# V's first weight slices over both DMA queues, with tile 1's steps one place earlier, in a fused attention and MLP block

## The chip, the cores and the metric

The kernel runs on one core of one Trainium2 chip. The metric is the device time of one execution in microseconds (us). The time before is the median of three runs.

## The reference

The input `x` has 2048 rows of 1024 values in bf16. The kernel computes a layer normalization, a sliding-window attention with 32 heads of 32, and a dense layer pair with silu, both with a residual.

```python
def _A_ref(x, wqkv, wo):
    qkv = (x @ wqkv)...          # q, k, v: 32 heads of 32
    scores = q k^T * 32 ** -0.5  # kept where 0 <= i - j < 256
    o = softmax(scores) @ v
    return o @ wo
def _B_ref(x, w1, w2):           # 1024 -> 3584 -> 1024
    return silu(x @ w1) @ w2

h = x + _A_ref(_layernorm(x), wqkv, wo)
h2 = h + _B_ref(_layernorm(h), w1, w2)
```

## The kernel before

The rows are worked on in four blocks of 512, each of four tiles of 128 rows. The order of the instructions of each engine is written out by hand. For every block the q, k and v groups are matmuls of 128x128 weights against 512 columns, eight per group, into one accumulator bank. The attention of a block is woven between the groups of the next one. Then come the output projection (`wo_group`, L268), the first dense layer (`h1_group`, L695) and the second (L732).

The change touches the beginning. SyncE's queue loads tile 0 of `x` (x0), then the eight slices of V's weights (wv0 to wv7: 128 rows of `wqkv`, all 1024 columns of V, 256 KB each), with tiles 2 and 3 (x2, x3) behind slices 3 and 4, and then 1 MB of the weights of q. ScalarE's queue loads tile 1 (x1) alone. Every one of these tiles and slices is 256 KB. ScalarE's instructions, its transfers among them, are issued in the order in which the program gives them; the same holds for SyncE.

The first two tiles are not normalized before the matmuls of V. TensorE transposes the raw tile (`turn`, L471), and the mean is taken off in the copies out of PSUM. The mean of tile 0 comes in two halves, one from ScalarE (`neg_mean`, L458) and one from VectorE (L502). The first two column blocks of a tile are centred by VectorE before they are transposed (`center_first`, L475; `turn_mid`, L479) and copied out (`copy_mid`, L482: VectorE for tile 0, ScalarE for tile 1). For the other six, the mean is spread over a row by two matmuls (`spread_mean`, L467), copied to SBUF (L513 for tile 0, L531 for tile 1), and added in `center` (L486). The variances are taken by ScalarE beside it (`var_first`, L491), and the root is multiplied in when V is copied out (L558).

The matmuls of V for tiles 0 and 1 (`slices`, L522) follow the list `FIRST`. An entry `(j, k)` is tile `j` against slice `k`: two matmuls of 512 columns. The entry `(1,)` is `turn_mid`, `copy_mid` and `spread_mean` of tile 1 with the work of ScalarE and VectorE behind them. An entry of four values transposes half of tile 2. After the list come V of tiles 2 and 3 (L237), and then the q and k groups of the first block (L247).

The banks of the accumulators are drawn by a counter:

```python
def next_acc():
    acc_n[0] += 1
    return acc_banks[acc_n[0] % len(acc_banks)]
```

`acc_banks` holds four banks during the first stage, two afterwards (`del acc_banks[2:]`, L569), and six from the first dense layer on: the four new ones (`hacc`) lie where the attention's scores lay, which ScalarE reads with the exponentials of L312 and L313.

Of the kernel before, what the change touches and what calls it, by code (L numbers as in the profile page):

```python
# [39 lines left out]
]  # L40
SPLIT = [(0, 8), (8, 16), (16, 21), (21, 27), (27, 32)]
FIRST = [
    (0, 0), (0, 1), (0, 2), (1,), (0, 3), (1, 0), (1, 1), (1, 2), (1, 3),
    (0, 4), (1, 4), (0, 5), (1, 5), (0, 6), (1, 6), (2, 0, 4, "turn"), (0, 7), (2, 4, 8, "turn"), (1, 7),
]

# [2 lines left out]
def kernel(  # L49
# [10 lines left out]
    nc = tc.nc  # L60
# [3 lines left out]
    S, D = x2d.shape  # L64
# [4 lines left out]
    KT = D // P  # L69
# [29 lines left out]
    def view(region, off, *dims):  # L99
        n = 1  # L100
        for d in dims:
            n *= d
        ap = region[:, off:off + n]
        if len(dims) == 2:
            return ap.rearrange("p (a b) -> p a b", b=dims[1])
        if len(dims) == 3:
            return ap.rearrange("p (a b c) -> p a b c", b=dims[1], c=dims[2])
        return ap

    wqk = view(r_w, 0, KT, 2 * D)  # L110
    wv = view(r_w, 16384, KT, D)
# [20 lines left out]
    wqkv_v = A_wqkv.rearrange("(kt p) n -> p kt n", p=P)  # L132
# [5 lines left out]
    def load_x(b, j, queue=nc.sync):  # L138
        queue.dma_start(out=x_ring[(b % 2) * 4 + j], in_=x2d[(b * 4 + j) * P:(b * 4 + j + 1) * P, :])

    def load_wqkv(c0, parts=1, queues=(nc.sync,)):
        dst = wqk[:, :, c0:c0 + 512] if c0 < 2 * D else wv[:, :, c0 - 2 * D:c0 - 2 * D + 512]
        n = KT // parts
        for k in range(0, KT, n):
            queues[k // n % len(queues)].dma_start(out=dst[:, k:k + n, :], in_=wqkv_v[:, k:k + n, c0:c0 + 512])
# [8 lines left out]

    load_x(0, 0)
    load_x(0, 1, nc.scalar)
    for k in range(KT):
        nc.sync.dma_start(out=wv[:, k, :], in_=wqkv_v[:, k, 2 * D:3 * D])
        if k in (3, 4):
            load_x(0, k - 1)  # L160
    load_wqkv(0)

    ident = const.tile([P, P], BF16, name="ident")
# [60 lines left out]
    acc_n = [0]  # L224
# [6 lines left out]
    def v_group(b, j, c, copy, between=None, acc=None):  # L231
        if acc is None:
            acc = next_acc()
        for kt in range(KT):
            if between:
                between(kt)
            nc.tensor.matmul(acc, lhsT=lnT_b[b % 2][:, kt, j * P:(j + 1) * P], rhs=wv[:, kt, c * 512:(c + 1) * 512],  # L237
                             start=(kt == 0), stop=(kt == KT - 1))
        copy(out=v[:, b * 4 + j, c * 16:(c + 1) * 16, 0:DH], in_=acc.rearrange("p (h d) -> p h d", d=DH))
# [327 lines left out]
    v_group(0, 3, 0, act)  # L567
    v_group(0, 3, 1, act)
    del acc_banks[2:]  # L569

    ps_tp.__exit__(None, None, None)
    ps_sc = tc.tile_pool(name="ps_sc", bufs=1, space=bass.MemoryType.PSUM, reuse_waits="tile")
# [212 lines left out]
```

## Time and profile before

| | |
|---|---|
| median of 3 runs | 691.5 us (691.18 to 691.62) |
| the profiled execution's own time | 691.33 us |
| its span | 689.6 us |
| granted TensorE clock | 1.000 |
| TensorE busy | 685.2 us (99%) |
| DMA moved | 61.48 MB, mean 89 GB/s |

The span goes from the first to the last instruction; the time is a little longer than the span. A row of the timeline gives the start, the time taken, the engine, the line, the operation, what is written and read, how many instructions are merged in it, and in brackets the idle time ahead of it and what ended that. `SPq` and `ACTq` are the issues of transfers on the queues of SyncE and ScalarE, `PE` is TensorE, `PEld` its weight loads, `DVE` VectorE, `ACT` ScalarE. A row of the waits gives the engine, what it writes, the line, whom it waited for, and then the total, the number of times and the longest.

### The profile page before, as it was taken

What the parts mean: (1) busy time and instruction counts of PE and PEld (TensorE: products, weight loads), DVE (VectorE), ACT (ScalarE), POOL (GpSimd) and SP (SyncE); (2) the same over time, 40 slices, a digit from 0 to 9 for tenths busy, and PEclk for the clock granted to TensorE, in tenths of its full rate; (3) what the DMA queues carried; (4) which work ended last, traced back from release to release, by engine and by line L of the source; (5) the groups of instructions that cost most, each with busy time, mean ns of one, the idle gap of its engine ahead of it and who ended that gap; (6) DMA issues with size and microseconds to landing.
All of it is one profiled execution on the core that took longest, in us unless ns stands there. A gap on an engine that the chain in (4) does not pass through costs nothing.

```text
span 689.6 us, 14236 instructions
## 1 busy us (share of the span) xinstructions
PE 685.2 (99%) x6008; PEld 343.0 (50%) x6008; DVE 291.3 (42%) x612; ACT 244.7 (35%) x462; POOL 160.6 (23%) x295
## 2 busy tenths in 40 slices
PE   9999999999999999999999999999999999999998
PEld 4445555555555555544444444444444444444445
DVE  5267647744444459444316133343133251333111
ACT  7326666667666766421310033300133100233000
POOL 1016665576666656400000000000000000000000
DMA  8842241136241888881023310032300124100110
GB/s 274 260 64 69 43 93 47 30 58 185 73 129 36 249 229 245 181 301 63 26 88 111 85 39 0 1 91 70 84 0 1 26 91 91 38 1 1 30 39 24
DMA packets 77648, 61.48 MB, mean 89 GB/s; under 512 B 52496, under 2 KB 60688, under 8 KB 77584
## 3 DMA queue, kind: packets, MB, share of 16 engines
q1 hardware_dynamic: 77440, 60.31, 31.9%
q8 instruction: 47, 0.77, 0.5%
q10 hardware_dynamic: 144, 0.26, 0.1%
q14 instruction: 17, 0.14, 0.1%
HBM read 39.85 MB, written 8.39 MB: 70 GB/s over the span
## 4 chain that ended last, share of the span: by engine, by line
PE 97%; DMA 1%; DVE 0%; ACT 0%; SPq 0%; issue 0%
PE hacc L695 19%; PE hacc L732 18%; PE acc L247 17%; PE acc L732 10%; PE acc L695 9%; PE acc L237 7%; PE acc L268 6%; PE o_ps L380 5%; PE sc L300 3%; PE hacc L268 1%; PE sc L352 1%; DMA r_w<-in_A_wqkv_dram 1%; PE sc L326 1%; PE tp L237 1%; PE acc L522 0%; PE o_ps L522 0%
## 5 line engine op out<-in xcount | busy, mean ns | idle before, releaser
L370 POOL TENSOR_SCALAR_AFFINE_SELECT r_e<-r_e 128x512 bf16<-128x512 bf16 (+1 forms) x288 | 157.6, 562 | 124.2 <-ACT r_e L360 60.4
L732 PEld LDWEIGHTS <-r_a 128*128 128x128 bf16 x952 | 90.9, 98 | 103.0
L695 PEld LDWEIGHTS <-r_w 128*128 128x128 bf16 x896 | 87.4, 98 | 105.2 <-issue 0.5
L732 PE MATMUL hacc<-r_a 128*128 128x512 bf16 (+1 forms) x588 | 124.1, 371 | 0.0
L695 PE MATMUL hacc<-r_e,r_w 128*128 128x512 bf16 x456 | 100.9, 379 | 0.0
L312 ACT ACTIVATE r_e<-sc 128x768 bf16<-128x768 f32 x96 | 78.2, 814 | 47.9 <-PE sc L300 46.9
L247 PEld LDWEIGHTS <-r_w 128*128 128x128 bf16 x512 | 47.1, 98 | 55.0 <-issue 1.0
L732 PE MATMUL acc<-r_a 128*128 128x512 bf16 (+2 forms) x364 | 72.6, 358 | 0.0
L704 ACT ACTIVATE r_n<-acc 128x512 f32<-128x512 f32 x15 | 9.0, 597 | 162.0 <-PE acc L695 162.0
L249 DVE CAST r_a<-acc 128x512 bf16<-128x512 f32 x56 | 38.7, 692 | 56.8 <-PE acc L247 56.5
L247 PE MATMUL acc<-r_t,r_w 128*128 128x512 bf16 x256 | 59.6, 380 | 0.0
L247 PE MATMUL acc<-r_w 128*128 128x512 bf16 x256 | 57.8, 380 | 0.0
L380 PEld LDWEIGHTS <-r_e 128*128 128x128 bf16 x1440 | 47.4, 96 | 17.9
L747 DVE SCALAR_TENSOR_TENSOR r_t<-hacc,r_t 128x512 bf16<-128x512 f32 (+1 forms) x21 | 14.1, 672 | 90.5 <-PE hacc L732 90.5
L268 PE MATMUL acc<-r_o,r_a 128*128 128x512 bf16 x216 | 50.9, 380 | 0.2
L695 PE MATMUL acc<-r_e,r_w 128*128 128x512 bf16 x216 | 49.1, 379 | 0.0
L380 PE MATMUL o_ps<-r_a,r_e 128*128 128x33 bf16 x1440 | 48.1, 178 | 0.0
L313 ACT ACTIVATE r_e<-sc 128x256 bf16<-128x256 f32 x96 | 37.6, 392 | 0.0
L268 PEld LDWEIGHTS <-r_a 128*128 128x128 bf16 x256 | 23.4, 98 | 27.4 <-issue 0.7
L695 PE MATMUL hacc<-r_a,r_w 128*128 128x512 bf16 x152 | 34.6, 379 | 0.2 <-ACT r_e L313 0.2
L705 DVE SCALAR_TENSOR_TENSOR r_a<-r_a,hacc 128x512 bf16<-128x512 f32 x30 | 20.6, 687 | 31.2 <-ACT r_a L704 31.2
L705 DVE SCALAR_TENSOR_TENSOR r_a<-r_n,hacc 128x512 bf16<-128x512 f32 x27 | 18.6, 687 | 28.1 <-ACT r_n L704 28.1
(106 smaller groups left out, 536.9 us busy)
## 6 DMA issues: line engine op xcount, KB each, us to landing
r_w<-in_B_w_dram SPq DMA_DIRECT2D x8, 896.0 KB, 6.2
r_a<-in_B_w_dram SPq DMA_DIRECT2D x7, 1024.0 KB, 8.0
r_w<-in_A_wqkv_dram SPq DMA_DIRECT2D x4, 1024.0 KB, 8.4
h_dram<-r_t SPq DMA_DIRECT2D x16, 256.0 KB, 2.4
r_t<-h_dram SPq DMA_DIRECT2D x16, 256.0 KB, 2.9
out_dram<-r_t SPq DMA_DIRECT2D x31, 128.0 KB, 1.7
r_o<-in_A_x_dram SPq DMA_DIRECT2D x15, 256.0 KB, 3.8
r_e<-h_dram SPq DMA_DIRECT2D x3, 1024.0 KB, 5.6
```

The costliest lines, as they stand in the source:

```text
L237: nc.tensor.matmul(acc, lhsT=lnT_b[b % 2][:, kt, j * P:(j + 1) * P], rhs=wv[:, kt, c * 512:(c + 1) * 512], start=(kt == 0), stop=(kt == KT ...
L247: nc.tensor.matmul(acc, lhsT=wqk[:, kt, col0:col0 + P], rhs=lnT_b[b % 2][:, kt, :], start=(kt == 0), stop=(kt == KT - 1))
L249: copy(out=(qT, kT)[which][b][:, g, :], in_=acc)
L268: nc.tensor.matmul(acc, lhsT=qT[b][:, g, j * P:(j + 1) * P], rhs=wo[:, g, c * 512:(c + 1) * 512], start=(g == 0), stop=(g == G - 1))
L300: nc.tensor.matmul(sc[hh // 2][half * 64:half * 64 + 64, hh % 2, col:col + qb - qa], lhsT=kT[t // 4][r0:r0 + DH, g, k0:k0 + 64], rhs=qT[b] ...
L312: nc.scalar.activation(out=tri[:, :, :, 64:256], in_=both, func=ACT.Exp, scale=scale)
L313: nc.scalar.activation(out=e[:, 1024:1280].rearrange("p (h q) -> p h q", q=P), in_=bank[:, :, 192:320], func=ACT.Exp, scale=scale)
L370: nc.gpsimd.affine_select(out=dst, in_=src, pattern=[[0, n] for n in dst.shape[1:-1]] + [[sgn, P]], compare_op=ALU.is_ge if upper else ALU ...
L380: nc.tensor.matmul(o_ps[pair][:, qt * 2 + hh, 0:VW], lhsT=chunk_of(i, bank, piece, pair, hh), rhs=v[:, b * 4 + kt, g * 4 + pair * 2 + hh, ...
L695: nc.tensor.matmul(acc, lhsT=w1[:, kt, ft * P:(ft + 1) * P], rhs=ln2T[b][:, kt, :], start=(kt == 0), stop=(kt == KT - 1))
L705: nc.vector.scalar_tensor_tensor(out=gT[:, ft, :], in0=th, scalar=1.0, in1=acc, op0=ALU.add, op1=ALU.mult)
L732: nc.tensor.matmul(acc[:, 0:c1 - c0], lhsT=gT[:, ft, j * P:(j + 1) * P], rhs=w2[ft // 4][:, ft % 4, c0:c1], start=(ft == 0), stop=(ft == F ...
```

## The change

The eight slices and tiles 2 and 3 are dealt out to both queues: SyncE's has wv0, wv2, wv4, x3, wv6, wv7 behind x0, ScalarE's has wv1, wv3, x2, wv5 behind x1. In the list `FIRST`, the entry `(1,)` stands before `(0, 2)` instead of behind it, and `(1, 0)` before `(0, 3)`. The counter of the accumulators is moved on by one behind V's last group.

```diff
 FIRST = [
-    (0, 0), (0, 1), (0, 2), (1,), (0, 3), (1, 0), (1, 1), (1, 2), (1, 3),
+    (0, 0), (0, 1), (1,), (0, 2), (1, 0), (0, 3), (1, 1), (1, 2), (1, 3),
...
     load_x(0, 0)
     load_x(0, 1, nc.scalar)
-    for k in range(KT):
-        nc.sync.dma_start(out=wv[:, k, :], in_=wqkv_v[:, k, 2 * D:3 * D])
-        if k in (3, 4):
-            load_x(0, k - 1)
+    for queue, what in ((nc.sync, (0, 2, 4, "x3", 6, 7)), (nc.scalar, (1, 3, "x2", 5))):
+        for k in what:
+            if k in ("x2", "x3"):
+                load_x(0, int(k[1]), queue)
+            else:
+                queue.dma_start(out=wv[:, k, :], in_=wqkv_v[:, k, 2 * D:3 * D])
     load_wqkv(0)
...
     del acc_banks[2:]
+    acc_n[0] += 1
```

## The prediction

> **What bounds the kernel now.** I read the page first, then the chain of work that ended last in order of time, then the waits of TensorE.
>
> ```profile
> span 689.6 us, 14236 instructions
> PE 685.2 (99%) x6008; PEld 343.0 (50%) x6008; DVE 291.3 (42%) x612; ACT 244.7 (35%) x462; POOL 160.6 (23%) x295
> PE 97%; DMA 1%; DVE 0%; ACT 0%; SPq 0%; issue 0%
> ```
>
> TensorE is busy for 99% of the span and carries 97% of the chain. The change removes no matmul, so it can only move the start of the unbroken matmul stream, or one of the few holes in it. The chain shows where that stream starts:
>
> ```profile
> 2.19 4.74 DMA r_w<-in_A_wqkv_dram
> ...
> 6.97 0.38 PE acc L522
> 7.35 0.22 PE o_ps L522
> 7.56 0.11 PE tp L479 x2
> 7.67 0.11 PE tp L467 x2
> 7.79 0.24 PE acc L522
> 8.03 0.50 PE o_ps L522 x2
> ```
>
> The last thing that TensorE waits for is the third slice of V's weights (slice k=2, called wv2 below), which lands at 2.19 + 4.74 = 6.93 us. From then on a matmul of 512 columns takes 0.215 us of the chain (0.43 for two) with no step of another engine between. So whatever delays or advances the step (1,1) of the list, which starts at 8.58, moves the end of the kernel by as much: nothing later absorbs it. TensorE's only other wait on another engine, after the first instruction, is this one, far behind the stage changed:
>
> ```profile
> PE hacc L695 <- ACT r_e L313: 0.2, 1, 0.2
> ```
>
> **The transfers and their places.** Next I read the issues in the timeline, and asked the DMA view for each one's time from issue to landing (second fence: size, then us).
>
> ```profile
> 0.80 1.28 ACT L153 ACT_TABLE_LOAD   x1 [0.80 <-PEq L769]
> 0.81 0.40 SPq L139 DMA_DIRECT2D r_o<-in_A_x_dram  x1
> 1.13 0.42 ACTq L139 DMA_DIRECT2D r_o<-in_A_x_dram  x1
> 1.26 1.83 SPq L158 DMA_DIRECT2D r_w<-in_A_wqkv_dram  x4
> 3.14 0.43 SPq L139 DMA_DIRECT2D r_o<-in_A_x_dram  x1
> 3.61 0.52 SPq L158 DMA_DIRECT2D r_w<-in_A_wqkv_dram  x1
> 4.18 0.43 SPq L139 DMA_DIRECT2D r_o<-in_A_x_dram  x1
> 4.98 0.33 SPq L158 DMA_DIRECT2D r_w<-in_A_wqkv_dram  x1
> 6.30 0.33 SPq L158 DMA_DIRECT2D r_w<-in_A_wqkv_dram  x1
> 6.67 0.43 SPq L158 DMA_DIRECT2D r_w<-in_A_wqkv_dram  x1
> ```
>
> ```profile
> r_o<-in_A_x_dram SPq DMA_DIRECT2D x1, 256.0 KB, 2.6
> r_o<-in_A_x_dram ACTq DMA_DIRECT2D x1, 256.0 KB, 3.2
> r_w<-in_A_wqkv_dram SPq DMA_DIRECT2D x1, 256.0 KB, 3.7
> r_w<-in_A_wqkv_dram SPq DMA_DIRECT2D x1, 256.0 KB, 4.6
> r_w<-in_A_wqkv_dram SPq DMA_DIRECT2D x1, 256.0 KB, 4.7
> ```
>
> The landings are issue plus time: x0 0.81 + 2.6 = 3.41, x1 1.13 + 3.2 = 4.33, wv0 1.26 + 3.7 = 4.96. The four issues from 1.26 are 0.46 apart, so wv1 lands at 1.72 + 4.6 = 6.32 and wv2 at 2.19 + 4.7 = 6.89.
>
> Now the gaps. Eight issues go out unhindered: x0, x1, wv0 to wv3, x2, wv4. The ninth, x3, follows at once. The tenth, wv5, could go at 4.65 and goes at 4.98, when wv0 has landed (4.96). The eleventh, wv6, could go at 5.35 and goes at 6.30, when wv1 has landed (6.32, to the rounding). The twelfth, wv7, goes at 6.67 without a gap, before wv2 has landed (6.89). I read this as a rotation of eight places: a transfer waits until the one eight places ahead of it has landed. The skip at wv7 then means that its predecessor is not wv2 but x1, long landed. So x1, which went out over ScalarE's queue, holds a place in the same rotation, the fourth, behind x0, wv0 and wv1: the places are shared by both queues.
>
> **The change part by part.** The rest of the working needs the start of both tiles' chains:
>
> ```profile
> 3.47 0.63 ACT L458 ACTIVATE r_e<-r_o 128x512 bf16<-128x512 bf16 x1 [1.18 <-DMA r_o<-in_A_x_dram]
> 4.28 0.35 DVE L475 TENSOR_SCALAR r_e<-r_o,mean 128x256 bf16<-128x256 bf16 x1
> 4.39 1.06 ACT L458 ACTIVATE r_e<-r_o 128x1024 bf16<-128x1024 bf16 x1 [0.19 <-DMA r_o<-in_A_x_dram]
> 4.69 0.42 PE L479 MATMUL tp<-ident,r_e 128*128 128x128 bf16 x2
> 5.12 0.63 PE L471 MATMUL tp<-ident,r_o 128*128 128x128 bf16 x4
> 5.55 0.57 PE L522 MATMUL acc<-r_w 128*128 128x512 bf16 x1
> 5.57 1.15 ACT L491 ACTIVATE r_e<-r_o,mean 128x1024 bf16<-128x1024 bf16 x1
> 6.03 0.28 DVE L475 TENSOR_SCALAR r_e<-r_o,mean 128x256 bf16<-128x256 bf16 x1
> 6.33 0.38 PE L522 MATMUL acc<-r_w 128*128 128x512 bf16 x1
> 7.71 0.37 ACT L482 COPY r_w<-tp 128x256 bf16<-128x256 bf16 x1 [0.90 <-PE tp L479]
> 8.58 0.38 PE L522 MATMUL o_ps<-r_w 128*128 128x512 bf16 x1
> ```
>
> *Order of the list.* The pair of transposes, the copy and the mean of tile 1 go ahead of (0,2), and (1,0) ahead of (0,3). With landings as they are, (0,1) ends at 6.33 + 0.43 = 6.76; the pair and the spread mean take 0.23 (7.56 to 7.79), to 6.99, now in the hole before wv2 lands; (0,2) runs to 7.42; tile 1's copy takes 0.37 from about 7.08, to 7.45; (1,0) runs to 7.88 and (0,3) to 8.31. So (1,1) starts at 8.31 in place of 8.58: a gain of 0.27.
>
> *Accumulator counter.* The first group of L695 is the 119th draw, 119 mod 6 = 5, the last of the new banks, and it has to wait for the exponentials that still read there: the 0.2 above. As the 120th draw it takes the first old bank, emptied a whole matmul group before; the new banks come third. A gain of 0.2; nothing is late next, since the scores' banks then have two groups more.
>
> *Two queues.* ScalarE's queue now issues x1, wv1, wv3, x2 and wv5, and all of these stand in its program ahead of the first mean (ScalarE's 3.47 row). At 0.46 each from 1.13, five unhindered issues end at about 3.43: they just fit under x0's landing at 3.41 and cost nothing. Under the rotation they do not go unhindered. Twelve transfers share eight places, four of the twelve must wait, and which queue's they are follows from the order of the places. The trace of before has no second transfer on ScalarE's queue, so that order is my estimate: x1 keeps the fourth place (behind three of SyncE's) and from there the queues alternate: x0, wv0, wv2, x1, wv4, wv1, x3, wv3, then wv6, x2, wv7, wv5. So x2 is the tenth and waits for wv0; wv5 is the twelfth and waits for x1. That is a wait on ScalarE, and behind it is queued the whole first stage of ScalarE: both means, the variances, tile 1's copy. Behind the first mean stands tile 0's centring on VectorE, and behind that TensorE.
>
> The price: wv0 landed at 4.96, but now shares the engines with wv1 on the other queue. The spacing of two landings is 6.89 - 6.32 = 0.57, so 4.96 to 5.53 are its bounds; I take 5.2. Two issues of 0.43 follow, so the first mean starts at 6.06 instead of 3.47: 2.6 late. Centring, transposes and copy of tile 0 follow it, and the first matmul of L522 goes from 5.55 to about 8.14. From here, by the durations above, (0,0) and (0,1) run to 9.00, tile 1's pair and mean to 9.23, (0,2) to 9.66. ScalarE meanwhile does the second mean without a wait (the first takes 0.85 with its accumulator, to 6.9; this one 1.25, to 8.15), then the variance (1.25, to 9.4), and only then tile 1's copy, to 9.77. (1,0) runs from 9.8 to 10.23, (0,3) to 10.66. So (1,1) starts at 10.66 instead of 8.58: 2.1 later, the gain of the new order already inside. All weights have landed by then.
>
> *The clock of the matmuls.* Four transposes take 0.43 from 5.12 to 5.55, 0.107 each; two take 0.11 at 7.56, 0.055 each. TensorE therefore reached its full rate between those rows, after some 5 us of work. With ScalarE late, TensorE stands idle from 4.7 to 7.3, before that point. No row shows whether the full rate still comes at about 6.3. If it does, nothing is added; if the slow rate lasts until (0,2) is done, the 1.53 us of work from 8.14 to 9.66 takes twice as long, 1.5 more. I take 0.3, near the lower end, because most of the slow stretch (1.1 to 4.7) is unchanged. The Trainium skill, in "TensorE: Matmul & The Clock Gate", Part 1, says that the clock is set by activity in a free-running window of about 3.4 us; by that an idle 2.6 us could cost one window, and the added time, as an estimate from that figure, would be up to 1.7. The doubled spacing agrees with its two rates; the window itself no run here shows.
>
> *The sum.* 2.1 - 0.2 + 0.3 = 2.2 on the profiled execution's own 691.33 (its span 689.6 and 1.7 around it), which is 0.17 under the median of 691.5. That gives **693.5**, or +0.3%. About 0.2%, 1.4 us, is what a measurement of this kernel can tell from no change: the line lies at 692.9.
>
> **The rivals.** *No wait on ScalarE.* If its transfers take places among the first nine, the change does what it says: -0.27 - 0.2 = -0.5, so 690.9, no change that can be told. For it: the five issues fit under x0's landing. Against it: x1 stands fourth already, and the four behind it would have to pass with at most one of SyncE's between. If the second queue also brought wv1 forward from 6.32, the slow matmuls of (0,0) would bind at about 5.55 + 0.86 = 6.41, so no more than a few tenths are to be had. The Trainium skill ("DMA: Bandwidth & Descriptors", Issuing engines are not separate DMA queues) says that issuing from several engines saves only the sequencer's time to issue, the data run over the same 16 engines; by it the landings stay and the gain is the 0.5 alone. SyncE's gaps before 4.98 and 6.30 lie behind the slices that bind, which agrees.
>
> *A later place.* If ScalarE's queue is one place ahead, x2 is ninth and waits for x0 only, but wv5 is eleventh and waits for wv2, 6.89: the first mean starts at 7.3, 3.9 late, of which 3.4 reach (1,1) by the same steps (the new order and the second mean's wait take off 0.5). 3.4 - 0.2 = 3.2, so 694.5, and up to 696 at the slow rate.
>
> *A shorter wait.* x2 ninth and wv5 tenth: one issue behind wv0, 5.2 + 0.43 = 5.63, 2.2 late, 1.7 at (1,1), so 1.5 net: 692.8, just inside what cannot be told.
>
> **How the numbers follow.** The forecast has 0.55, the later place 0.2, the shorter wait 0.1, no wait 0.15. The forecast without the slow rate is 693.2, and with its worst 694.7: nearly all of it is slower by over 0.2%, but a landing of wv0 at 4.96 would make 693.0, close to the line, so I give 0.05 of it to no change. Slower 0.5 + 0.2 = 0.70; within 0.05 + 0.1 + 0.11 = 0.26; faster 0.04, for a gain of the no-wait case that I cannot name. The range 691.9 to 695.3 leaves out the no-wait case and the slow end of the later place.
>
> **What would show it.** Right: in the changed profile ScalarE's queue has an issue of L139 or L158 that starts after 4.9 with a gap before it, the first mean (L458) starts at about 6, the first L522 matmul at about 8.1, and L695 no longer waits for L313. Wrong: five issues on ScalarE's queue back to back until 3.5, and the first mean still near 3.5.

## The result and the profile after

The changed kernel takes 694.9 us (median of 6 runs, 693.72 to 695.31), the kernel before 691.5 (6 runs, 691.13 to 691.84): a ratio of 1.0049, with a 95% interval of 1.0038 to 1.0059. It is 3.4 us slower where 2.0 over that median were forecast. The profiled execution took 695.23 us with a span of 693.5, 3.9 more than before.

First the chain of the changed kernel in order of time, from its first transfer of weights on (start, time, what):

```profile
1.26 3.86 DMA r_w<-in_A_wqkv_dram
5.12 0.02 issue
5.14 0.33 ACTq L139
5.47 0.04 issue
5.51 0.45 ACTq L162
5.97 0.05 issue
6.01 0.73 ACT r_e L460 x2
6.75 0.03 issue
6.77 0.36 DVE r_e L477
...
7.78 0.43 PE tp L473 x4
8.21 0.43 PE acc L524
8.63 0.43 PE o_ps L524
...
12.47 0.68 PE o_ps L524 x2
13.15 0.22 PE acc L524
...
18.13 3.45 PE tp L239 x16
```

The chain passes through wv0 (issued at 1.26), then two issues on ScalarE's queue (x2, L139, and wv5, L162), then the first mean (L460), VectorE's centring (L477) and the matmuls of V (L524). Before, it came straight from wv2 to the matmuls. The last line is the first group behind the list, whose row before was:

```profile
13.94 3.45 PE tp L237 x16
```

It starts 4.2 us later. From there on both kernels take the same but for 0.3 us: 693.5 - 18.1 = 675.4 against 689.6 - 13.9 = 675.7. So the loss lies in the first 18 us, and the longest waits there say whose it is (two of the waits in the first 25 us of the changed kernel, the longest of ScalarE and the longest of TensorE):

```profile
ACT r_e L460 <- DMA r_w<-in_A_wqkv_dram: 3.7, 1, 3.7
...
PE tp L481 <- DVE r_e L477: 2.3, 1, 2.3
```

ScalarE stood 3.7 us ahead of the first mean, for a transfer of weights that the mean does not read; in the kernel before it stood 1.2 us there, for x0. The rows of the issues and their times to landing show the rotation at work:

```profile
3.81 0.33 SPq L162 DMA_DIRECT2D r_w<-in_A_wqkv_dram  x1
5.14 0.33 ACTq L139 DMA_DIRECT2D r_o<-in_A_x_dram  x1
6.56 0.33 SPq L162 DMA_DIRECT2D r_w<-in_A_wqkv_dram  x1
```

```profile
r_o<-in_A_x_dram SPq DMA_DIRECT2D x1, 256.0 KB, 3.0
r_w<-in_A_wqkv_dram SPq DMA_DIRECT2D x1, 256.0 KB, 3.9
r_w<-in_A_wqkv_dram SPq DMA_DIRECT2D x1, 256.0 KB, 4.8
```

x0 lands at 0.81 + 3.0 = 3.81, and wv6 goes out at 3.81. wv0 lands at 1.26 + 3.9 = 5.16, and x2 goes out at 5.14. wv2 lands at 1.73 + 4.8 = 6.53, and wv7 goes out at 6.56. These are the ninth, tenth and eleventh places of the order that the prediction wrote down. The matmuls of L524 between 8.2 and 12.5 are 0.43 us apart, from 13.15 on 0.22: the second part of the loss, half the rate for TensorE.

### The profile page after: what moved, and what is told of

It is laid out like the page before. It is cut to its first block, busy times and chain, and to the rows that moved or that the text cites. A ratio compares the mean times of both kernels' runs of the same rounds, so it can differ in the third digit from the quotient of the medians.

```text
span 693.5 us, 14234 instructions
## 1 busy us (share of the span) xinstructions
PE 687.1 (99%) x6008; PEld 343.5 (50%) x6008; DVE 290.8 (42%) x612; ACT 244.5 (35%) x462; POOL 160.6 (23%) x295
## 4 chain that ended last, share of the span: by engine, by line
PE 96%; DVE 2%; DMA 2%; SPq 0%; issue 0%; ACTq 0%; ACT 0%; DVEq 0%
PE hacc L698 19%; PE acc L249 16%; PE hacc L735 14%; PE acc L735 14%; PE acc L698 8%; PE acc L239 7%; PE acc L270 5%; PE o_ps L382 5%; PE sc L302 2%; PE hacc L270 1%; DMA h_dram<-r_t 1%; PE sc L354 1%; PE o_ps L524 1%; PE acc L524 1%; DMA r_w<-in_A_wqkv_dram 1%; DVE r_t L272 1%
## 5 line engine op out<-in xcount | busy, mean ns | idle before, releaser
L698 PE MATMUL hacc<-r_e,r_w 128*128 128x512 bf16 x480 | 106.0, 379 | 0.0
L735 PE MATMUL hacc<-r_a 128*128 128x512 bf16 (+1 forms) x504 | 100.6, 361 | 0.0
L735 PE MATMUL acc<-r_a 128*128 128x512 bf16 (+1 forms) x448 | 95.0, 372 | 0.0
L707 ACT ACTIVATE r_n<-hacc 128x512 f32<-128x512 f32 x30 | 17.9, 597 | 178.9 <-PE hacc L698 178.9
L270 PE MATMUL acc<-r_o,r_a 128*128 128x512 bf16 x208 | 49.1, 380 | 0.2
L698 PE MATMUL acc<-r_e,r_w 128*128 128x512 bf16 x192 | 43.4, 379 | 0.0
L750 DVE SCALAR_TENSOR_TENSOR r_t<-acc,r_t 128x512 bf16<-128x512 f32 (+1 forms) x16 | 10.6, 664 | 69.3 <-PE acc L735 69.3
L708 DVE SCALAR_TENSOR_TENSOR r_a<-r_n,hacc 128x512 bf16<-128x512 f32 x30 | 20.6, 688 | 33.1 <-ACT r_n L707 33.1
L750 DVE SCALAR_TENSOR_TENSOR r_t<-hacc,r_t 128x512 bf16<-128x512 f32 (+1 forms) x18 | 11.6, 646 | 51.3 <-PE hacc L735 51.3
```

Of the source, the lines that this page charges most:

```text
L270: nc.tensor.matmul(acc, lhsT=qT[b][:, g, j * P:(j + 1) * P], rhs=wo[:, g, c * 512:(c + 1) * 512], start=(g == 0), stop=(g == G - 1))
L698: nc.tensor.matmul(acc, lhsT=w1[:, kt, ft * P:(ft + 1) * P], rhs=ln2T[b][:, kt, :], start=(kt == 0), stop=(kt == KT - 1))
L708: nc.vector.scalar_tensor_tensor(out=gT[:, ft, :], in0=th, scalar=1.0, in1=acc, op0=ALU.add, op1=ALU.mult)
L735: nc.tensor.matmul(acc[:, 0:c1 - c0], lhsT=gT[:, ft, j * P:(j + 1) * P], rhs=w2[ft // 4][:, ft % 4, c0:c1], start=(ft == 0), stop=(ft == F ...
L750: nc.vector.scalar_tensor_tensor(out=t_out[j % 2][:, c0:c1], in0=acc[:, 0:c1 - c0], scalar=0.5, in1=t_in[j % 2][:, c0:c1], op0=ALU.mult, o ...
```

## The experiments

Theory A: the shared rotation holds ScalarE, and the slow rate of the matmuls behind the idle stretch doubles the damage. Rival B: two queues side by side make the slices land later. Rival C: late slices make the spacing of the matmuls. Rival D: the new order of the list costs something.

**The hold taken away (e1).** ScalarE's queue keeps wv1 and wv3, all within eight places.

```diff
-    for queue, what in ((nc.sync, (0, 2, 4, "x3", 6, 7)), (nc.scalar, (1, 3, "x2", 5))):
+    for queue, what in ((nc.sync, (0, 2, 4, "x2", "x3", 5, 6, 7)), (nc.scalar, (1, 3))):
```

> The changed kernel with x2 and wv5 moved back to SyncE's queue, so that ScalarE's queue has x1, wv1 and wv3 alone, all within the first eight places of the rotation. Theory A (the tenth and twelfth places, shared by both queues, hold ScalarE until wv0 has landed; the slow matmul clock behind the idle stretch adds to it): no wait on ScalarE's queue, first mean at about 3.5, first L524 matmul at about 5.6, time 690.6 to 691.2. Rival B (two queues side by side make the slices land later, and the wait is only a sign of it): the first slices still land late, and it stays slower than before by 1 us or more, 692.5 to 694.

691.29 us against 691.34 before on the same chip, ratio 0.9999 (0.9990 to 1.0007). The hold is gone, the first mean starts at 3.62, and with it goes the whole loss. But the gain that A had promised beside it (690.6 to 691.2) is not there.

**One issue fewer behind the wait (e6).**

```diff
-    for queue, what in ((nc.sync, (0, 2, 4, "x3", 6, 7)), (nc.scalar, (1, 3, "x2", 5))):
+    for queue, what in ((nc.sync, (0, 2, 4, "x3", 5, 6, 7)), (nc.scalar, (1, 3, "x2"))):
```

> The changed kernel with wv5 alone moved back to SyncE's queue: x2 is still the tenth transfer and waits for wv0, and one issue of 0.45 us fewer stands between that landing and the first mean. Theory A: x2 issued at about 5.1, first mean at about 5.5 instead of 6.0, first matmul of V 0.45 earlier than in the changed kernel, time between 692.3 and 694.8 by the clock. Rival B: no difference from the changed kernel, as as many bytes go out over both queues.

693.15 us, ratio 1.0028 (1.0018 to 1.0039). x2 still goes out at 4.95, when wv0 has landed, and the mean starts at 5.33, 0.7 before the changed kernel's: one issue (0.5) and wv0's earlier landing (0.2). The loss is 1.8 us in place of 3.4; 0.7 of the difference is the mean; the rest fits a shorter spell of the half rate, which here shows in the granted clock too. Its windows (us; busy time and count of PE, PEld, DVE, ACT, POOL; granted clock, DMA share, GB/s):

```profile
0.00:8.00 8.00, 5.14 (x24) 2.77 (x24) 2.60 (x13) 4.09 (x7) 2.96 (x7) 0.99 0.79 277
8.00:14.00 6.00, 6.00 (x24) 2.74 (x24) 4.05 (x13) 4.70 (x11) 0.00 (x0) 0.73 0.91 320
```

A granted clock of 0.73 over 6 us is half rate for 54% of it, 3.2 us. Its chain shows where, by the four transposes (x4) and the matmuls:

```profile
6.98 0.22 PE tp L473 x4
...
7.98 0.41 PE o_ps L524
8.39 0.21 PE tp L481 x2
...
10.95 0.66 PE o_ps L524 x2
11.61 0.21 PE acc L524
```

At 6.98 the full rate had been granted (four in 0.22); at 8 it was taken back, and it returned at about 11.4. So the half rate began after the work had begun again, behind an idle stretch of 1.7 us. Whether the idle stretch is its cause is what e5 tests.

**TensorE kept busy (e5).** Two scratch matmuls fill the idle stretch; the hold stays.

```diff
     turn(1, 2 * P, 1, 2, 4)
+    for n in (4, 2):
+        busy(n)
```

> The changed kernel with two scratch matmuls (f32, as the two at the start; 1.7 and 0.85 us at the slow rate) in the stretch in which TensorE stands idle from 4.7 to 7.2 us; nothing reads what they write. Theory A (about half of the loss is the clock, which falls behind because TensorE stands idle): the matmuls of V are 0.215 us apart from about 8.0 or soon after, step (1,1) starts at 10.7 to 11.0 instead of 12.7, time 693.0 to 693.4. Rival C (the 0.43 us spacing comes from slices that land late, or from contention of weights and transfers): the spacing stays, 694.5 to 695.5.

692.29 us, ratio 1.0015 (1.0006 to 1.0024). The first mean is as late as ever (5.78), yet the loss falls from 3.4 us to 0.95, more than A had forecast (693.0 to 693.4). The chain has four transposes in 0.22 and the first matmuls of V (here L526) 0.22 apart, and the granted clock stays whole:

```profile
7.44 0.22 PE tp L473 x4
7.66 0.34 PE acc L526
8.01 0.22 PE o_ps L526
```

```profile
8.00:14.00 6.00, 5.95 (x31) 2.51 (x29) 4.32 (x14) 4.82 (x11) 0.00 (x0) 1.00 0.97 344
```

This settles rival C: the spacing is gone, though the slices land about as they did (wv7, which follows wv2's landing, goes out at 6.40, against 6.56 in the changed kernel). Of the 3.4 us, about 2.4 went with the filler and 1 is left, the hold less the small gains. The 2.4 are not the spell behind 8 us alone: the transposes ahead of it ran at the full rate too, and wv0 landed 0.2 us earlier in this execution.

**The queues alone (e4).** The changed kernel with the old order and no step of the counter.

```diff
-    (0, 0), (0, 1), (1,), (0, 2), (1, 0), (0, 3), (1, 1), (1, 2), (1, 3),
+    (0, 0), (0, 1), (0, 2), (1,), (0, 3), (1, 0), (1, 1), (1, 2), (1, 3),
...
-    acc_n[0] += 1
```

> The changed kernel with the old order of the list and without the step of the counter: the two queues alone. Theory A: all of the loss is here; first mean at 6.0 as in the changed kernel, the wait of L697 for the exponentials back (0.2), time 694 to 695.6, no faster than the changed kernel by more than its own spread. Rival D (the order of the list costs something, as tile 1's pair now waits on ScalarE ahead of (0,2)): 692 to 693.5.

694.67 us, ratio 1.0048 (1.0034 to 1.0061): all of the loss, and rival D falls. The 0.2 us wait for the exponentials is back. The half rate has the picture of e6: the four transposes of L473 at the full rate, the matmuls at half of it from about 8.3 to 11.6, with a granted clock of 0.72 from 8 to 14.

**The hold alone (e9).** All transfers on SyncE's queue; ScalarE is made to wait by one activation that reads a column of wv1.

```diff
+    nc.scalar.activation(out=dummy[:], in_=wv[:, 1, 0:1], func=ACT.Identity)
     neg_mean(mean[:, 6:7], x_ring[0][:, 512:1024])
```

> The hold without the queues: the kernel of e8 (all transfers on SyncE's queue, new order, counter moved on) with one more instruction on ScalarE ahead of the first mean, an activation on one column of wv1 whose result nothing reads, so that ScalarE is held until that slice has landed, at 5.8 to 6.3. Theory A (the hold and the clock behind it are the loss, whatever the queues do): first mean at 6.1 to 6.6, first matmul of V at 8.1 to 8.6, the matmuls 0.43 us apart for some us, time 692.5 to 695. Rival B (most of the loss is that the slices land later over two queues): less than 1.5 us over e8, under 691.7.

694.32 us, ratio 1.0048 (1.0035 to 1.0062), 3.8 over its base without the activation (690.51 on the same chip). Its rows have the picture of the changed kernel:

```profile
6.14 0.20 ACT L501 ACTIVATE dummy<-r_w 128x1 f32<-128x1 bf16 x1 [3.85 <-DMA r_w<-in_A_wqkv_dram]
6.25 0.61 ACT L458 ACTIVATE r_e<-r_o 128x512 bf16<-128x512 bf16 x1
```

```profile
8.00:14.00 6.00, 6.00 (x26) 2.62 (x24) 4.67 (x15) 5.18 (x13) 0.00 (x0) 0.72 0.99 343
```

Here too the transposes at 7.7 run at the full rate and the matmuls from 8.4 to 11.6 at half of it. So the hold and the rate make the loss without a second queue. Theory A stands.

**The order alone (e2) and the counter alone (e3)**, each on the kernel before:

> The kernel before with the new order of the list alone. Theory A: tile 1's pair and mean fill the hole before wv2 lands; (1,1) starts at 8.31 instead of 8.58; 0.27 us faster, 691.2. Rival D (the order costs): 691.6 or more.

> The kernel before with the step of the accumulator counter alone. Theory A: the 0.2 us wait of L695 for the exponentials is gone and nothing comes in its place: 691.3. Rival E (the wait only moves to the first group that draws a new bank, or a wait of the copies of the first block comes in): 691.5 or more.

The order: 691.07 us, ratio 1.0000 (0.9991 to 1.0009). The counter: 690.48, ratio 0.9994 (0.9985 to 1.0004). Neither can be told from no change by itself. In the profile of e3 the wait for the exponentials is gone and no wait of a group of L695 came in its place.

**Both, on one queue (e8)**, the first two of three measurements:

```diff
-    (0, 0), (0, 1), (0, 2), (1,), (0, 3), (1, 0), (1, 1), (1, 2), (1, 3),
+    (0, 0), (0, 1), (1,), (0, 2), (1, 0), (0, 3), (1, 1), (1, 2), (1, 3),
...
     del acc_banks[2:]
+    acc_n[0] += 1
```

> The kernel before with the new order and the step of the counter, and the transfers on SyncE's queue as before. Theory A: the sum of both, 0.47 us faster: 691.0. If the gains are not additive (the same stall hidden twice): 691.2 to 691.4.

> The kernel of e8 once more, for the comparison with e9 and e10 on the same chip: 0.5 to 1 us under the kernel before, 690.2 to 690.8.

690.21 us, ratio 0.9990 (0.9981 to 0.9999), and 690.51, ratio 0.9987 (0.9979 to 0.9996): 0.6 to 0.9 us under the kernel before, where 0.47 had been forecast. Both intervals lie below 1, by very little.

**Two queues without a hold, beside one queue (e1 again and e8 a third time, on one chip).** e1 should have matched e8, as they have the same order and counter, and it did not.

> The kernel of e1 beside that of e8 on one chip: they differ only in where the transfers go out (wv1 and wv3 on ScalarE's queue or all on SyncE's; no wait on ScalarE in either). If two queues side by side make wv1 and wv3 land later (e1: 6.89 and 8.06; e8: 5.83 and 7.37), e1 is 0.5 to 1.1 us slower than e8. If those landings were chance, both are alike within 0.3.

> The other half of that comparison: 0.5 to 1 us under the kernel before, wv1 landed by 6.3 and wv3 by 7.6.

691.63 us (ratio 1.0002, 0.9993 to 1.0011) against 690.68 (0.9991, 0.9982 to 1.0000): 0.95 us between the medians. The two intervals still touch, but e1 and e8 had differed the same way on another chip (691.29 and 690.21), and the profiles agree with the times. The rows of the matmuls of V, first two queues, then one:

```profile
6.85 0.38 PE L524 MATMUL acc<-r_w 128*128 128x512 bf16 x1 [0.59 <-DMA r_w<-in_A_wqkv_dram]
...
8.06 0.38 PE L524 MATMUL acc<-r_w 128*128 128x512 bf16 x1 [0.39 <-DMA r_w<-in_A_wqkv_dram]
```

```profile
6.39 0.38 PE L522 MATMUL acc<-r_w 128*128 128x512 bf16 x1
...
7.04 0.38 PE L522 MATMUL acc<-r_w 128*128 128x512 bf16 x1
```

These are (0,1) and (0,2). With two queues wv1 lands at 6.79 and wv2 at 8.03, and TensorE waits for both; with one they land at 5.73 and 6.40 and it waits for neither. The landings differ between executions of the same kernel: in e1's first profile they were 6.9 and 7.1, and TensorE waited 0.2 us; over the three profiles of e8, wv1 landed at 5.7 to 5.8 and wv2 at 6.4 to 6.8. So rival B names a real cost, about 1 us in this comparison, but not that of the changed kernel, where wv1 and wv2 landed at 5.9 and 6.5, ahead of the first matmul of V at 8.0.

The rotation shows here without a hold: in e1 the eleventh transfer, wv6, goes out when wv2, the third, lands (7.12 in the first profile, 8.03 in the second).

**x3 ahead of wv4 (e10)**, on e8:

```diff
-        if k in (3, 4):
-            load_x(0, k - 1)
+        if k == 3:
+            load_x(0, 2)
+            load_x(0, 3)
```

> The kernel of e8 with x3 loaded ahead of wv4 instead of behind it. In e8 the chain passes through x3: landed at 9.39, its statistics on VectorE, and behind them the norm of tile 2 that TensorE's transposes need. If that is the next bound, x3 lands 0.7 earlier and up to 0.3 us are gained, 689.9 to 690.2. If wv4, which now lands at 9.4 and is needed at about 9.2, binds instead: 690.3 to 690.6.

690.60 us, ratio 0.9992 (0.9983 to 1.0001), beside 690.51 of e8 on the same chip: no gain, as the second of its two forecasts had it. In its profile (0,2) waits 0.3 us for wv2, which lands at 7.10 there; x3 goes out at 3.62 but lands at 9.1, hardly earlier than in e8's second profile (9.2).

## Why the prediction was right or wrong

**Right: the rotation, the places and the direction.** The order of the places was an estimate from one gap of 0.04 us ahead of wv7. The measured 694.9 lies closer to the 694.5 of the later place than to the forecast, but the trace rules that rival out: there x2 would go out behind x0 and wv5 behind wv2. The changed profile has x2 behind wv0 and wv7 behind wv2, as written. The first mean was put at 6.06 and started at 6.01; the first matmul of V was put at 8.14 and started at 8.00. e9 shows that holding ScalarE alone is enough. A small misreading did no harm: ScalarE's mean and variance were put at 0.85 and 1.25 us, and their rows are 0.76 and 1.2 apart (6.01, 6.77, 7.95), but tile 1's copy then waited for TensorE.

**Mis-sized: the rate.** The term was 0.3 us, with 1.5 as its worst. Step (1,1) was put at 10.66 and came at 12.70; the ten matmuls and four small steps ahead of it took 4.7 us from 8.00 instead of 2.5, so the term measured 2.2. Two things were wrong. The worst case stopped the half rate at (0,2), for which no row spoke; it lasted to about 13. And the early work from 1.1 to 4.7 us was taken as credit, while e6, e4 and e9 show the rate granted and then taken back behind the idle stretch, and e5, where TensorE is kept busy there, has no such spell. With 2.2 in place of 0.3 the sum is 695.4, beside the profiled 695.23. The median of 694.9 lies beyond the 694.7 that the forecast gave as its own worst; that it still lies inside the range is luck, as the range had room for the later place. The Trainium skill ("TensorE: Matmul & The Clock Gate", Part 1) gives a window of about 3.4 us; e6's half rate lasted about that long (8.0 to 11.4), which agrees. The same part of the Trainium skill puts the idle state behind at least one idle window of that length, and here the measurement differs: TensorE was idle for 1.7 us in e6. In the changed kernel the half rate shows in the four transposes at 7.78 (0.43) and lasts to 13, longer than one such window; no row of its profile has the full rate before that. Of its six runs two have a mean granted clock of 0.998, as in the profiles of e4, e6 and e9, and four have 1.000, as in its own profile, so both pictures seem to occur. That the rate comes and goes at other moments from run to run would explain the spread from 693.72 to 695.31, which is larger than before's; the single times were not traced, so this stays an inference.

**Right in direction, size not shown: order and counter.** 0.27 and 0.2 were forecast. The sum was measured at 0.6 to 0.9 (e8), more than the two, with intervals that reach from 0.0 to 1.5. Alone, the order had 0.06 and the counter 0.65 between the medians, and neither can be told from nothing.

**Wrong: the price of the rival without a wait.** It said that the landings stay as they are, and gave 690.9. e1 had 691.29 and 691.63, no better than before. The landings did not stay: in the two profiles of e1 wv1 and wv2 came later than in the three of e8, wv2 at 8.03 instead of 6.40 in the direct comparison. That the slices needed first share the engines with later ones of the other queue is the likely reason; no row shows the sharing itself. The rule of the Trainium skill ("DMA: Bandwidth & Descriptors", Issuing engines are not separate DMA queues), that such transfers interleave on the same engines, pointed there, and the prediction read it only as "no gain".

## What to carry to other kernels

Before giving a compute engine's queue more transfers, count all transfers in flight over all queues: where a shared set of places runs out, the engine stands still for a transfer that it doesn't need, and all its work behind it is late. Price an idle stretch of TensorE early in a kernel at more than its length: here TensorE idled for 2.3 us, and scratch matmuls in that stretch took back 2.4 of the 3.4 us lost. Two queues did not make the slices land sooner here that are needed in order: without a hold they cost about 1 us beside one queue.

## What the runs showed that was not expected

The rate can be granted and then taken back after the work has resumed: in e6 the transposes at 6.98 ran at the full rate, and the matmuls from 7.98 to about 11.4 at half, and e4 and e9 have the same. And the moment at which it is first granted moves between executions of nearly the same start. In the second profile of e8 the four raw transposes of tile 1 and the first matmul read

```profile
4.84 0.39 PE L471 MATMUL tp<-ident,r_o 128*128 128x128 bf16 x4
5.18 0.39 PE L522 MATMUL acc<-r_w 128*128 128x512 bf16 x1
```

against 0.63 and 0.57 for the same rows before: in e8 the full rate had come more than a microsecond earlier.

The granted clock of the record doesn't always show the half rate. In the changed kernel it stands at 1.00 where the matmuls are 0.43 us apart:

```profile
8.00:13.00 5.00, 5.00 (x18) 2.08 (x17) 3.73 (x11) 3.99 (x8) 0.00 (x0) 1.00 1.02 340
```

In e6 and e9 the stretch from 8 to 14 has 0.73 and 0.72. The record also reads 1.00 for the first 5.5 us of the kernel before, where four transposes take 0.43. In these traces it falls below 1.00 only where the full rate had been seen before; that this is the rule is not shown. The spacing of like matmuls is the safer reading.
